# Folding a per-head matrix into projection weights: products of 120 rows by 128 columns, and quarters of 60 by 64

## The chip, the cores and the metric

The kernel runs on one core of a Trainium2 chip. The metric is the device time of one execution in microseconds (us). Engines are named as in the profile: PE is TensorE (PEld its weight loads), DVE is VectorE, ACT is ScalarE, POOL is GpSimd, SP is SyncE, which issues the DMAs.

## What is computed

Two layers, each a linear attention and a dense block, on x of 2048 rows by 640 columns with 32 heads of 20. Of the reference, what matters here:

```python
q, k, v = split(layernorm(x) @ wqkv)              # per head: S x 20
pq = einsum("bhsd,hdf->bhsf", q, w_phi)           # the same 20 x 20 matrix per head
pk = einsum("bhsd,hdf->bhsf", k, w_phi)           # for queries and for keys
phi_q = concat([softmax(pq), softmax(-pq)])       # phi_k likewise
o = phi_q (phi_k^T v) / (phi_q phi_k^T 1 + 1e-6)
x = x + o @ wo
x = x + mish(layernorm(x) @ w1 + b1) @ w2
```

Since `(n @ W) @ w_phi` is `n @ (W @ w_phi)`, the kernel multiplies w_phi into the query and key weights once, at the start of the first layer. Softmax does not change when a constant is taken off a row, so the last of the 20 columns of each head is subtracted from the other 19 (`DL` = 19), and 32 x 19 = 608 columns are left.

## The kernel before, in words

**Blocks.** x is worked in 8 blocks of 256 rows, two tiles of 128 each. For each block the first attention stage makes keys (`k0`, `k1`), values (`v0`, `v1`) and queries (`q0`, `q1`), each by `project`: for each of five 128-row slices of the weights three F32R products (high x high, high x low, low x high), in two halves of columns. Every weight is therefore held as a rounded high part and a low part, the rest.

**The folds.** `load_raw` loads the transposed query or key weights as six tiles: t = 0 to 3 with 120 rows (six heads), t = 4 and 5 with 80 (four heads). `fold_part` (L248) multiplies, for slice k and tile t, the 120 x 128 piece of raw weights with the block-diagonal w_phi (`bd`) in F32; three tiles t fill one bank of PSUM, c = 0 with 18 heads and c = 1 with 14. `fold_end` takes a bank out: ACT rounds it to the high part (L261), DVE subtracts to get the low part (L262), 342 columns for c = 0 and 266 for c = 1. `shift_phi` (L255, POOL) does the subtraction of the last column in `bd`. There are 5 x 6 products for queries and as many for keys (`fold_phi`).

**The value weights.** They are loaded by `fetch_v` (L183) and split by ACT (L140, high) and DVE (L141, low part, 640 columns), one slice after another: slices 0 to 4.

**The statistics.** `norm_stats` takes, for each tile of an x block, two BNStats (L281, 320 columns each) and an aggregate (L283); POOL and DVE make scale and offset (L290, L291, L293). ACT normalizes (L129, L132), PE transposes (L311), ACT and DVE make high and low parts (L129 or L132, L317).

**After a projection** of queries or keys, `features` copies it out (L132), reduces maximum and minimum per head (L400), subtracts (L401, L403), takes Exp on ACT (L132), sums per head on DVE (L409), inverts (L410) and multiplies on POOL (L411). Queries are then transposed by DVE (L456) and stored (L460). The products of keys and values are L448.

**What sets the order.** The first stage, up to the query projection of tile 0 and the splits of the values, is written out by hand (`with written():` in `attend_first`): the order of these instructions among themselves on each engine is the program's. All else is placed by a planner, which puts each instruction in its engine's queue by its own model of times; it can put an instruction of its own between those written by hand. Each engine then runs its queue strictly in that order. All loads and stores go through one queue, SP's, and take turns on eight completion semaphores: in the built program each waits until the DMA eight places before it has landed. Two PSUM tags are used here: `mm` (two banks, 2 buffers) and `one` (one bank, 4 buffers).

Of the kernel before, what the change touches and what calls it, by code (L numbers as in the profile page):

```python
# [8 lines left out]
F32 = mybir.dt.float32  # L9
F32R = mybir.dt.float32r  # L10
AF = mybir.ActivationFunctionType
ALU = mybir.AluOpType
# [4 lines left out]
P = 128  # L17
S = 2048
D = 640
F = 1536  # L20
H = 32
DH = 20
DL = DH - 1
KD = D // P
# [7 lines left out]
QK = H * DL  # L32
# [3 lines left out]
VW = H * (DH + 1)  # L36
SKEW = 2
LAYERS = 2
LN_EPS = 1e-5
DEN_EPS = 1e-6  # L40
E_CAP = 65536.0
# [3 lines left out]
def kernel(  # L45
# [13 lines left out]
    nc = tc.nc  # L59
# [3 lines left out]
    wts = ctx.enter_context(tc.tile_pool(name="wts", bufs=1))  # L63
# [116 lines left out]
    def fetch_v(k):  # L180

        st = (row_tile, row_tile, v_tile, v_tile, big_tile)[k]()[:, :D]
        nc.sync.dma_start(st, wv[k * P:(k + 1) * P, :])  # L183
        return st
# [42 lines left out]
    def load_raw(which, ts=range(6)):  # L227

        raw = []
        for t in ts:  # L230
            rows = 120 if t < 4 else 80
            if t < 5:
                r = wts.tile([P, D], F32, tag=f"r2{'hl'[which]}{5 + t}", name=f"raw{which}{t}")
            else:
                r = r2_wide(10 + which, F32)[:, 0]

            n = P if t < 5 else rows
            c0 = which * D + (t * 120 if t < 5 else D - rows)
            nc.sync.dma_start(r[:n], wqk_t[c0:c0 + n, :])
            raw.append((r, rows))  # L240
        return raw

    def fold_part(ps, k, t, bd, raw):

        r, rows = raw[t]
        heads = rows // DH
        n = DL * (6 * (t % 3) if t < 5 else 10)
        nc.tensor.matmul(ps[:, n:n + heads * DL].rearrange("p (j d) -> p j d", d=DL), r[:rows, k * P:(k + 1) * P],  # L248
                         bd[:rows, t, :rows].rearrange("p (j d) -> p j d", d=DH)[:, :, :DL], start=True, stop=True)

    def shift_phi(bd, ts):

        b = bd[:, ts].rearrange("p t (j d) -> p (t j) d", d=DH) if isinstance(ts, slice) else (
            bd[:80, ts, :80].rearrange("p (j d) -> p j d", d=DH))
        nc.gpsimd.tensor_tensor(b[:, :, :DL], b[:, :, :DL], b[:, :, DL:].to_broadcast([b.shape[0], b.shape[1], DL]),  # L255
                                op=ALU.subtract)

    def fold_end(ws, ps, k, c):
        n0, n1 = (0, 18 * DL) if c == 0 else (18 * DL, QK)
        hi, lo = ws[k][0][:, n0:n1], ws[k][1][:, n0:n1]  # L260
        nc.scalar.activation(hi, ps[:, :n1 - n0], AF.Copy)  # L261
        nc.vector.tensor_tensor(lo, ps[:, :n1 - n0], hi.bitcast(F32), op=ALU.subtract)  # L262

    def fold_phi(ws, bd, raw):

        pss = {}
        for k, c in ((0, 0), (1, 0), (2, 0), (3, 0), (0, 1), (1, 1), (2, 1), (3, 1), (4, 0), (4, 1)):
            if c == 0:
                mm = None if k % 2 else mm_tile()
                pss[k] = [one_tile(), one_tile()] if k % 2 else [mm[:, 0], mm[:, 1]]  # L270
            ps = pss[k][c]
            for t in range(3 * c, 3 * c + 3):
                fold_part(ps, k, t, bd, raw)
            fold_end(ws, ps, k, c)


    def norm_stats(t, xt):
# [136 lines left out]
    def fetch(x_src, b, xt=None):  # L414
        xt = x_tile() if xt is None else xt
        nc.sync.dma_start(xt, row_block(x_src, b))
        return xt

    def attend_first(layer, x_src, first):
# [58 lines left out]
        if first is None:  # L478
            with written():
                xt = fetch(x_src, 0)  # L480
                bd = big_tile()[:120, :720].rearrange("p (t c) -> p t c", t=6)
                nc.sync.dma_start(bd[:, :3], phi_bd[:, :3])
                raw_q = load_raw(0, range(3))

                nc.vector.memset(bd[:80, 5, :80], 0.0)
                nc.sync.dma_start(bd[:40, 5, :40], phi_bd[80:120, 4, 80:120])
                nc.sync.dma_start(bd[40:80, 5, 40:80], phi_bd[:40, 5, :40])
                nc.sync.dma_start(bd[:, 3:5], phi_bd[:, 3:5])
                shift_phi(bd, slice(0, 3))
                raw_q += load_raw(0, range(3, 6))  # L490
                kv_ws = [r1_pair(k) for k in range(KD)]
                raw_v = [fetch_v(k) for k in range(KD)]
                raw = load_raw(1)
                early = fetch(x_src, 1)
                mvs = [norm_stats(t, xt) for t in range(BT)]
                norm_scale(0, mvs)
                shift_phi(bd, slice(3, 5))
                shift_phi(bd, 5)

                q_ws = [r2_pair(k) for k in range(KD)]  # L500
                mm = [mm_tile(), mm_tile()]
                pcs = [mm[0][:, 0], mm[0][:, 1], mm[1][:, 0], mm[1][:, 1], one_tile()]
                for t in range(3):
                    for k in range(KD - 1):
                        fold_part(pcs[k], k, t, bd, raw_q)
                fold_end(q_ws, pcs[0], 0, 0)
                xn = [row_tile() for _ in range(BT)]
                act(xn[0], xt[:, 0, :], AF.Identity, bias=stats[:, 0, 1, 0:1], scale=stats[:, 0, 0, 0:1])
                nc.vector.tensor_scalar(xn[1], xt[:, 1, :], stats[:, 0, 0, 1:2], stats[:, 0, 1, 1:2],
                                        op0=ALU.mult, op1=ALU.add)  # L510
                fold_end(q_ws, pcs[1], 1, 0)
                fold_end(q_ws, pcs[2], 2, 0)
                nxt = Transposed(xn)
                nxt.step()
                fold_end(q_ws, pcs[3], 3, 0)
                nxt.step()
                for t in range(3):
                    fold_part(pcs[4], 4, t, bd, raw_q)
                nxt.step()
                fold_end(q_ws, pcs[4], 4, 0)  # L520
                mm = mm_tile()
                q0 = [mm[:, 0], mm[:, 1], mm]
                project_half(q0[0], nxt, 0, q_ws, 0, 0, w=QC)

                def make_v(k):
                    split(kv_ws[k][0][:, D:2 * D], kv_ws[k][1][:, D:2 * D], raw_v[k])

                for k in range(KD):
                    ps = one_tile()
                    for t in range(3, 6):  # L530
                        fold_part(ps, k, t, bd, raw_q)
                    fold_end(q_ws, ps, k, 1)
                    if k > 0:
                        make_v(k - 1)
                project_half(q0[1], nxt, 0, q_ws, 0, 1, w=QC)
                make_v(KD - 1)
            nc.sync.dma_start(mask, bass.AP(tensor=head_mask.tensor, offset=head_mask.offset,
                                            ap=[[1, 120], [120 * (DH + 1), 3]]))
        else:
            nxt, kv_ws = first  # L540
            load_k_weights(kv_ws)
            q_ws = load_q_weights()
        for b in range(NB):
# [351 lines left out]
    with tc.block(schedule_with_timeline_sim=True):  # L895
        src, first = x, None
        for layer in range(LAYERS):
            last = layer == LAYERS - 1
            dst = out if last else x2_d
# [39 lines left out]
            src = dst  # L939
# [38 lines left out]
```

## Time and profile before

| | us |
|---|---|
| median of three runs (1368.06 to 1368.76) | 1368.17 |
| the profiled execution | 1368.56 |
| its span | 1366.8 |
| PE busy | 1351.2 |
| DVE busy | 1075.5 |
| ACT busy | 578.4 |
| POOL busy | 452.6 |

In rows of groups the columns are line, engine, operation, tile written and tiles read, shape and count, then busy time and the mean in ns of one, then the idle time of the engine ahead of them and what ended it. In rows of the timeline they are start, length, engine, line and instruction, and in brackets the idle time before it. Starts are counted from the start of the span. Products overlap on PE, so the difference of two starts says more than a length.

### The profile page before, as it was taken

The page shows a single profiled execution, that of the slowest core. Times are in us where ns is not written, and L with a number is a line of the kernel's source. Part 1 is how long each engine was busy: PE and PEld are TensorE (multiplying, and loading weights), DVE is VectorE, ACT ScalarE, POOL GpSimd, SP SyncE. Part 2 cuts the span into 40 slices and gives each one's busy share as a digit, 9 for nine tenths or more (in the row PEclk, how much of TensorE's full clock was granted, in tenths as well). Part 3 has the DMA queues.
Part 4 walks back from the last instruction along what each step waited for, and adds up shares of the span by engine and source line. Part 5 has one row for each costly group of instructions (what it writes and reads, how often), then busy time and mean ns, then how long its engine had stood idle before and what let it go on. Part 6 is the DMA issues. An engine that isn't in the chain of part 4 may idle for free. (4 is left out here: it accounts for less than half of the span.)

```text
span 1366.8 us, 30959 instructions
## 1 busy us (share of the span) xinstructions
PE 1351.2 (99%) x12896; PEld 1337.9 (98%) x12896; DVE 1075.5 (79%) x1822; ACT 578.4 (42%) x970; POOL 452.6 (33%) x401
## 2 busy tenths in 40 slices
PE   9999999999999999999999999999999999999998
PEld 9999999999999999999999999999999999999998
DVE  6888988876787888778769898989668776677775
ACT  5444444212454544455444333432235444444443
POOL 2355554434222222122235444544252211111112
PEclk9999999999999999999999999999999999999999
DMA  9533333798714443334563433458974221333200
GB/s 343 150 81 64 74 60 78 213 282 273 223 36 93 116 117 84 57 94 113 151 218 75 83 60 70 86 132 267 287 251 136 78 71 35 90 97 97 77 21 20
DMA packets 350469, 169.19 MB, mean 124 GB/s; under 512 B 287209, under 2 KB 323801, under 8 KB 350329
## 3 DMA queue, kind: packets, MB, share of 16 engines
q1 hardware_dynamic: 350329, 167.22, 45.4%
q8 instruction: 101, 1.65, 0.5%
q14 instruction: 39, 0.32, 0.1%
HBM read 104.59 MB, written 62.59 MB: 122 GB/s over the span
## 5 line engine op out<-in xcount | busy, mean ns | idle before, releaser
L816 PE MATMUL mm<-r2h,ol 128*128 128x320 f32 x1280 | 304.9, 309 | 0.0
L800 POOL TENSOR_TENSOR ol<-big,ol 128x512 fp32r<-128x512 f32 (+1 forms) x98 | 131.2, 1338 | 477.2 <-ACT ol L799 419.1
L774 PE MATMUL one<-xtl,r1h 128*128 128x256 f32 x960 | 268.2, 279 | 0.0
L774 PE MATMUL one<-xth,r1l 128*128 128x256 f32 x960 | 268.0, 279 | 0.0
L774 PE MATMUL one<-xth,r1h 128*128 128x256 f32 x960 | 265.9, 279 | 0.0
L816 PEld LDWEIGHTS mm<-r2h,ol 128*128 128x128 f32 x1280 | 219.2, 188 | 0.0
L816 PE MATMUL mm<-r2l,ol 128*128 128x320 f32 x640 | 197.3, 309 | 0.0
L375 PE MATMUL mm<-r1h,xth 128*128 128x304 f32 (+1 forms) x600 | 185.4, 309 | 2.2 <-DVE r1l L262 1.5
L375 PE MATMUL mm<-r1h,xtl 128*128 128x304 f32 (+1 forms) x600 | 183.6, 307 | 2.0 <-DVE xtl L317 1.8
L375 PE MATMUL mm<-r1l,xth 128*128 128x304 f32 (+1 forms) x600 | 183.8, 306 | 0.0
L774 PEld LDWEIGHTS one<-xtl,r1h 128*128 128x128 f32 x960 | 180.4, 188 | 0.0
L774 PEld LDWEIGHTS one<-xth,r1l 128*128 128x128 f32 x960 | 180.4, 188 | 0.0
L774 PEld LDWEIGHTS one<-xth,r1h 128*128 128x128 f32 x960 | 179.6, 188 | 0.0
L789 DVE TENSOR_SCALAR big<-big 128x512 f32<-128x512 f32 (+1 forms) x98 | 56.9, 581 | 110.2 <-ACT big L787 110.0
L411 POOL TENSOR_TENSOR r<-r,r 128x1280 f32<-128x1280 f32 x32 | 79.1, 2473 | 131.7 <-DVE r L410 124.1
L816 PEld LDWEIGHTS mm<-r2l,ol 128*128 128x128 f32 x640 | 120.2, 188 | 0.0
L791 ACT ACTIVATE big<-big,two 128x512 f32<-128x512 f32 (+1 forms) x98 | 70.2, 716 | 116.2 <-DVE big L790 116.2
L787 ACT ACTIVATE big<-one,b1s 128x256 f32<-128x256 f32 x192 | 80.9, 468 | 88.8 <-PE one L774 88.3
L799 ACT ACTIVATE ol<-big 128x512 fp32r<-128x512 f32 (+1 forms) x98 | 60.9, 622 | 134.5 <-DVE big L798 134.4
L375 PEld LDWEIGHTS mm<-r1h,xth 128*128 128x128 f32 x600 | 112.8, 188 | 3.9 <-DVE r1l L262 1.7
L375 PEld LDWEIGHTS mm<-r1h,xtl 128*128 128x128 f32 x600 | 112.7, 188 | 2.7 <-DVE xtl L317 2.7
L375 PEld LDWEIGHTS mm<-r1l,xth 128*128 128x128 f32 x600 | 112.8, 188 | 0.1
(136 smaller groups left out, 3125.0 us busy)
## 6 DMA issues: line engine op xcount, KB each, us to landing
e_d<-r SPq DMA_DIRECT2D x128, 160.0 KB, 4.0
big<-e_d SPq DMA_DIRECT2D x32, 640.0 KB, 7.4
x_d<-xt SPq DMA_DIRECT2D x23, 640.0 KB, 4.6
xt<-x_d SPq DMA_DIRECT2D x22, 640.0 KB, 5.5
n_d<-xn SPq DMA_DIRECT2D x176, 80.0 KB, 2.2
xt<-in_x SPq DMA_DIRECT2D x16, 640.0 KB, 4.0
xn<-x_d SPq DMA_DIRECT2D x28, 320.0 KB, 4.4
v<-n_d SPq DMA_DIRECT2D x30, 256.0 KB, 3.0
```

What stands on the lines that cost most here:

```text
L375: nc.tensor.matmul(ps[:, :w], a[:, sl], r, start=(k == 0 and n == 0), stop=(k == KD - 1 and n == 2))
L411: nc.gpsimd.tensor_tensor(eg, eg, r.unsqueeze(2).to_broadcast([P, 2 * H, DH]), op=ALU.mult)
L774: nc.tensor.matmul(ph[:, j, :], l, r, start=(n == 0), stop=(n == 3 * KD - 1))
L787: exps[0] = nc.scalar.activation(part(ta, 0)[:, j - js.start], ph[:, j, :], AF.Exp, bias=b1s[:, 2 * pr + j:2 * pr + j + 1]).ins
L789: nc.vector.tensor_scalar_min(e, e, E_CAP)
L791: nc.scalar.activation(r, n, AF.Ln, bias=two)
L799: nc.scalar.activation(ah[:, js], n, AF.Copy)
L800: nc.gpsimd.tensor_tensor(al[:, js], n, ah[:, js].bitcast(F32), op=ALU.subtract)
L816: nc.tensor.matmul(pys[t][:, c, :HC], l[:, j, sl], r, start=(f == 0 and n == 0), stop=(f == KF - 1 and n == 2))
```

## The change

The 30 products each of queries and keys become 30 sets of four: two slots s of at most three heads (60 rows), at rows 0 and 64 of the raw tile, and two halves q of 64 columns. The four use the four 64 x 64 quarters of the array. Slot s writes bank s of a pair, half q writes partitions 64q to 64q + 63.

- `FOLD` lists, for each tile t, first head and number of heads of both slots.
- `load_raw` loads two times 64 rows for each t (for the last key tile 64 and 40): 12 loads in place of 6.
- `load_phi` loads w_phi as blocks of 60 x 60 (fewer heads at the end) into `bd`, which is zeroed first (128 x 360): 4 loads for c = 0 and 6 for c = 1, in place of 1 and 3.
- `pair_banks` takes two `one` banks or one `mm` tile in turn. `fold_end` takes out an `mm` pair by one instruction each on ACT and DVE (342 or 266 columns) and two `one` banks by two each (171 or 133).
- `shift_phi` is two instructions of 9 x 19 columns in place of 18 x 19, 12 x 19 and 4 x 19.

The orders of the built programs differ only in the first stage and the folds of the keys; from the second key projection (`k1` of block 0) on, PE's are the same. On DVE, from the first low part of the queries' c = 1 on (st = BNStats, ag = aggregate, of the x block whose number follows; lq = low part of queries, slice k; sv = split of values; lk = low part of keys; a number after x is how many pieces):

```
before: lq0 lq1 sv0 lq2 sv1 lq3 sv2 lq4 sv3 sv4 lk(0,0) st1x4 ag1x2 st2x2 max,min(q0) st2x2 ...
after:  lq0x2 lq1 sv0 lq2x2 st1x3 sv1 st1 ag1 lq3 sv2 ag1 st2x2 lq4x2 sv3 st2x2 sv4 ag2 ... max,min(q0) ... st3x4 sum(q0) lk(0,0) ...
```

On PE, before, the three products of the first key fold stand among the last query folds and the rest between `v1` and the key projection of tile 0, the last inside it; after, all ten groups stand between `v1` and that projection, and the transposes of x block 1 behind them.

The diff, cut to its core:

```diff
+FOLD = (((0, 3), (9, 3)), ((3, 3), (12, 3)), ((6, 3), (15, 3)), ((18, 3), (25, 3)), ((21, 3), (28, 2)), ((24, 1), (30, 2)))
...
-            n = P if t < 5 else rows
-            c0 = which * D + (t * 120 if t < 5 else D - rows)
-            nc.sync.dma_start(r[:n], wqk_t[c0:c0 + n, :])
+            for s, (h, _) in enumerate(FOLD[t]):
+                c0 = which * D + h * DH
+                n = min(64, 2 * D - c0)
+                nc.sync.dma_start(r[64 * s:64 * s + n], wqk_t[c0:c0 + n, :])
...
+    def load_phi(bd, c):
+        def block(s, t, h, n, m=1):
...
+        for args in (((0, 0, 0, 3, 2), (0, 2, 6, 3), (1, 0, 9, 3), (1, 1, 12, 3, 2)) if c == 0 else
+                     ((0, 3, 18, 3), (1, 3, 25, 3), (0, 4, 21, 3), (1, 4, 28, 2), (0, 5, 24, 1), (1, 5, 30, 2))):
+            block(*args)
...
     def fold_part(ps, k, t, bd, raw):
-        nc.tensor.matmul(ps[:, n:n + heads * DL].rearrange("p (j d) -> p j d", d=DL), r[:rows, k * P:(k + 1) * P],
-                         bd[:rows, t, :rows].rearrange("p (j d) -> p j d", d=DH)[:, :, :DL], start=True, stop=True)
+        for s, (h, heads) in enumerate(FOLD[t]):
+            n0 = DL * (h % 9 if t < 3 else h - 18 - 7 * s)
+            rows = slice(64 * s, 64 * s + max(2, heads) * DH)
+            rhs = bd[rows, t, :heads * DH].rearrange("p (j d) -> p j d", d=DH)[:, :, :DL]
+            for q in range(2):
+                nc.tensor.matmul(ps[s][64 * q:64 * q + 64, n0:n0 + heads * DL].rearrange("p (j d) -> p j d", d=DL),
+                                 raw[t][rows, k * P + 64 * q:k * P + 64 * q + 64], rhs, start=True, stop=True)
...
     def fold_end(ws, ps, k, c):
+        if len(ps) > 2:
+            parts = [(slice(n0, n0 + 2 * w), ps[2][:, :, :w])]
+        else:
+            parts = [(slice(n0 + s * w, n0 + (s + 1) * w), ps[s][:, :w].unsqueeze(1)) for s in range(2)]
+        for cs, src in parts:
+            n = src.shape[1]
+            hi, lo = (ws[k][i][:, cs].rearrange("p (s d) -> p s d", s=n) for i in range(2))
+            nc.scalar.activation(hi, src, AF.Copy)
+            nc.vector.tensor_tensor(lo, src, hi.bitcast(F32), op=ALU.subtract)
...
     def fold_phi(ws, bd, raw):
-        for k, c in ((0, 0), (1, 0), (2, 0), (3, 0), (0, 1), (1, 1), (2, 1), (3, 1), (4, 0), (4, 1)):
+        for k in range(KD):
+            for c in range(2):
+                ps = pair_banks((k + c) % 2)
...
-                bd = big_tile()[:120, :720].rearrange("p (t c) -> p t c", t=6)
-                nc.sync.dma_start(bd[:, :3], phi_bd[:, :3])
+                bd = big_tile()[:, :360].rearrange("p (t c) -> p t c", t=6)
+                nc.vector.memset(bd, 0.0)
+                load_phi(bd, 0)
                 raw_q = load_raw(0, range(3))
+                load_phi(bd, 1)
+                shift_phi(bd, 0)
                 raw_q += load_raw(0, range(3, 6))
```

More of the change, by code (lines that the diff above doesn't have):

```diff
@@ L230, in load_raw @@
         for t in ts:
-            rows = 120 if t < 4 else 80
-            if t < 5:
-                r = wts.tile([P, D], F32, tag=f"r2{'hl'[which]}{5 + t}", name=f"raw{which}{t}")
-            else:
-                r = r2_wide(10 + which, F32)[:, 0]
-            n = P if t < 5 else rows
-            c0 = which * D + (t * 120 if t < 5 else D - rows)
-            nc.sync.dma_start(r[:n], wqk_t[c0:c0 + n, :])
-            raw.append((r, rows))
-        return raw
-    def fold_part(ps, k, t, bd, raw):
[L245 to L248, printed above, removed]
-                         bd[:rows, t, :rows].rearrange("p (j d) -> p j d", d=DH)[:, :, :DL], start=True, stop=True)
@@ L251, in shift_phi @@
[L251 to L256, printed above, removed]
-    def fold_end(ws, ps, k, c):
[L259 to L262, printed above, removed]
@@ L264, in fold_phi @@
-    def fold_phi(ws, bd, raw):
-        pss = {}
-        for k, c in ((0, 0), (1, 0), (2, 0), (3, 0), (0, 1), (1, 1), (2, 1), (3, 1), (4, 0), (4, 1)):
[L268 to L274, printed above, removed]
+            r = (wts.tile([P, D], F32, tag=f"r2{'hl'[which]}{5 + t}", name=f"raw{which}{t}") if t < 5 else
+                 r2_wide(10 + which, F32)[:, 0])
@@ new lines, in load_raw @@
+            for s, (h, _) in enumerate(FOLD[t]):
+                c0 = which * D + h * DH
+                n = min(64, 2 * D - c0)
+                nc.sync.dma_start(r[64 * s:64 * s + n], wqk_t[c0:c0 + n, :])
+            raw.append(r)
+        return raw
+    def load_phi(bd, c):
+        def block(s, t, h, n, m=1):
+            a, j = divmod(h, 6)
+            src = phi_bd[DH * j:DH * (j + n), a, DH * j:DH * (j + n)]
+            dst = bd[64 * s:64 * s + DH * n, t:t + m, :DH * n]
+            if m > 1:
+                step = 60 * (phi_bd.ap[0][0] + 1) if j == 0 else None
+                src = bass.AP(tensor=src.tensor, offset=src.offset, ap=[src.ap[0], [step, m], src.ap[-1]])
+                nc.sync.dma_start(dst, src)
+            else:
+                nc.sync.dma_start(dst[:, 0], src)
+        for args in (((0, 0, 0, 3, 2), (0, 2, 6, 3), (1, 0, 9, 3), (1, 1, 12, 3, 2)) if c == 0 else
+                     ((0, 3, 18, 3), (1, 3, 25, 3), (0, 4, 21, 3), (1, 4, 28, 2), (0, 5, 24, 1), (1, 5, 30, 2))):
+            block(*args)
@@ new lines, in shift_phi @@
+    def shift_phi(bd, c):
+        b = bd[:, 3 * c:3 * c + 3].rearrange("p t (j d) -> p (t j) d", d=DH)
+        nc.gpsimd.tensor_tensor(b[:, :, :DL], b[:, :, :DL], b[:, :, DL:].to_broadcast([P, 9, DL]), op=ALU.subtract)
+    def fold_end(ws, ps, k, c):
+        n0, w = (0, 9 * DL) if c == 0 else (18 * DL, 7 * DL)
+        if len(ps) > 2:
[7 more added lines that the diff above has]
+            nc.vector.tensor_tensor(lo, src, hi.bitcast(F32), op=ALU.subtract)
@@ L277, in norm_stats, with pair_banks @@
+    def pair_banks(single):
+        if single:
+            return [one_tile(), one_tile()]
+        mm = mm_tile()
+        return [mm[:, 0], mm[:, 1], mm]
+    def fold_phi(ws, bd, raw):
+        for k in range(KD):
+            for c in range(2):
+                ps = pair_banks((k + c) % 2)
+                for t in range(3 * c, 3 * c + 3):
+                    fold_part(ps, k, t, bd, raw)
+                fold_end(ws, ps, k, c)
     def norm_stats(t, xt):
@@ L480, in attend_first @@
                 xt = fetch(x_src, 0)
-                bd = big_tile()[:120, :720].rearrange("p (t c) -> p t c", t=6)
-                nc.sync.dma_start(bd[:, :3], phi_bd[:, :3])
+                bd = big_tile()[:, :360].rearrange("p (t c) -> p t c", t=6)
+                nc.vector.memset(bd, 0.0)
+                load_phi(bd, 0)
                 raw_q = load_raw(0, range(3))
[L485 to L489, printed above, removed]
+                load_phi(bd, 1)
+                shift_phi(bd, 0)
                 raw_q += load_raw(0, range(3, 6))
@@ L496, in attend_first @@
                 norm_scale(0, mvs)
-                shift_phi(bd, slice(3, 5))
-                shift_phi(bd, 5)
+                shift_phi(bd, 1)
                 q_ws = [r2_pair(k) for k in range(KD)]
-                mm = [mm_tile(), mm_tile()]
-                pcs = [mm[0][:, 0], mm[0][:, 1], mm[1][:, 0], mm[1][:, 1], one_tile()]
+                pcs = [pair_banks(k < 2) for k in range(KD - 1)]
                 for t in range(3):
@@ L516, in attend_first @@
                 nxt.step()
+                ps = pair_banks(True)
                 for t in range(3):
-                    fold_part(pcs[4], 4, t, bd, raw_q)
+                    fold_part(ps, KD - 1, t, bd, raw_q)
                 nxt.step()
-                fold_end(q_ws, pcs[4], 4, 0)
+                fold_end(q_ws, ps, KD - 1, 0)
                 mm = mm_tile()
@@ L528, in attend_first @@
                 for k in range(KD):
-                    ps = one_tile()
+                    ps = pair_banks(k % 2 == 0)
                     for t in range(3, 6):
```

## The prediction

> **What bounds the kernel now.** I read the page first, then the groups of the first 45 us, then the timeline of each engine there, since everything that the change touches lies before 45 us.
>
> ```profile
> PE 1351.2 (99%) x12896; PEld 1337.9 (98%) x12896; DVE 1075.5 (79%) x1822; ACT 578.4 (42%) x970; POOL 452.6 (33%) x401
> ```
>
> PE is busy for 1351.2 of 1366.8 us. After the first stage it has next to no idle time to give, so what that stage gains or loses reaches the end undiminished. The groups of TensorE in the first 45 us:
>
> ```profile
> L248 PE MATMUL mm<-big,raw 120*128 120x114 f32 (+1 forms) x54 | 7.5, 277 | 0.2 <-DVE r1l L262 0.2
> L248 PE MATMUL one<-big,raw 120*128 120x114 f32 (+1 forms) x46 | 6.7, 273 | 0.0
> ...
> L92 PE MATMUL one<-ident 128*128 128x128 f32 x30 | 5.6, 371 | 1.3 <-POOL ident masks.py:199 1.3
> ...
> L375 PE MATMUL mm<-r1h,xth 128*128 128x304 f32 x10 | 3.1, 313 | 1.5 <-DVE r1l L262 1.5
> ...
> L311 PE MATMUL one<-ident,xn 128*128 128x128 f32 x20 | 3.1, 278 | 0.9 <-ACT xn L129 0.9
> L248 PE MATMUL one<-big,r 80*128 80x76 f32 x14 | 2.7, 275 | 0.0
> L248 PE MATMUL mm<-big,r 80*128 80x76 f32 x6 | 1.2, 275 | 0.0
> ```
>
> The folds are L248: 54 + 46 + 14 + 6 = 120 records for 60 products in F32, so each product is two instructions. PE idles only 0.9 and 1.5 us there, both times for another engine.
>
> **The products.** The rate is read from starts, not durations, since products overlap:
>
> ```profile
> 29.91 0.82 PE L248 MATMUL one<-big,raw 120*128 120x114 f32 x6
> 30.57 0.83 PE L248 MATMUL mm<-big,raw 120*128 120x114 f32 x6
> ...
> 64.50 0.83 PE L448 MATMUL one<-big,v 128*21 128x40 f32 x64
> 65.26 0.66 PE L311 MATMUL one<-ident,xn 128*128 128x128 f32 x4
> ...
> 252.72 1.38 PE L652 MATMUL mm<-kvb,big 120*64 120x63 f32 x40
> 253.94 0.27 PE L652 MATMUL mm<-kvb,ol 80*64 80x42 f32 x4
> 254.03 1.36 PE L652 MATMUL mm<-kvb,big 120*64 120x63 f32 x40
> ```
>
> Three products take 30.57 - 29.91 = 0.66 us, or 0.22 each, and all 60 take 13.2. L652 writes two halves of 64 columns in turn: 44 instructions in 254.03 - 252.72 = 1.31 us, so 0.060 for a product that two tiles share. L448 writes four column tiles in turn: 64 instructions in 0.76 us, so 0.024 per product. Cost falls with the number of column tiles; row tiles side by side are in no row here. If four quarters run at once, a set of four costs two turns of L652's pair, 2 x 0.060 = 0.12 us; if only the two column halves do, 4 x 0.060 = 0.24. All 60 sets then cost 7.2 or 14.4 us: a gain of 6.0 or a loss of 1.2. I take 7.2, since L448 shows that more tiles give more.
>
> [...]
>
> **Does that gain reach the end?** It would if PE bounded the whole stage. The built order of instructions says otherwise. VectorE now, from the timeline:
>
> ```profile
> 17.55 0.82 DVE L141 TENSOR_TENSOR r1l<-xn,r1h 128x640 fp32r<-128x640 f32 x1 [0.19 <-ACT r1h L140]
> ...
> 20.45 0.43 DVE L262 TENSOR_TENSOR r2l<-one,r2h 128x266 fp32r<-128x266 f32 x1
> 20.79 0.82 DVE L141 TENSOR_TENSOR r1l<-v,r1h 128x640 fp32r<-128x640 f32 x1
> 21.52 0.82 DVE L141 TENSOR_TENSOR r1l<-big,r1h 128x640 fp32r<-128x640 f32 x1
> 22.26 0.51 DVE L262 TENSOR_TENSOR r1l<-mm,r1h 128x342 fp32r<-128x342 f32 x1
> 23.10 1.67 DVE L281 BATCH_NORM_STATS2 bn<-xt 128x6 f32<-128x320 f32 x4 [0.33 <-DMA xt<-in_x]
> ```
>
> L141 is the low part of the value weights, five "splits", done at 21.52 + 0.82 = 22.34. Only then come the statistics L281 of x block 1, which waited 0.33 us for their load. In the changed kernel the planner sets three of these statistics **ahead of split 1** (counting from 0), and two of block 2 ahead of split 3 and two ahead of split 4. VectorE runs in order: when it comes there, at about 18.6 (split 0 ends at 18.37, then one low part), it holds until x block 1 has landed. Behind it stand the low parts of queries 3 and 4 and splits 1 to 4, which PE needs for the rest of q, v0 and v1.
>
> **When does that load land?** It is the 23rd load in SyncE's queue now and the 41st after.
>
> ```profile
> DMA  0036999999999999999999999999999999999999
> ...
> 0.72 0.39 SPq L416 DMA_DIRECT2D xt<-in_x  x1
> 1.17 0.47 SPq L482 DMA_DIRECT2D big<-in_phi_bd  x1
> 1.69 1.29 SPq L239 DMA_DIRECT2D raw<-in_wqk_t  x3
> ...
> 8.92 0.90 SPq L183 DMA_DIRECT2D v<-in_wv  x2
> ...
> 10.35 3.35 SPq L239 DMA_DIRECT2D raw<-in_wqk_t  x5
> 14.20 0.33 SPq L239 DMA_DIRECT2D r<-in_wqk_t  x1
> 15.02 0.33 SPq L416 DMA_DIRECT2D xt<-in_x  x1
> ```
>
> The first row is the DMA load over 0 to 25 us in 40 slices: full from 3 us on. From the start to that x block the shapes give 6.94 MB now and 6.96 after (phi blocks 0.16 less, the last tiles of q and k 0.18 more), so it lands no earlier for its bytes: 23.07 now. More loads can only delay it. Each issue holds SyncE for some 0.44 us (two in 0.90, three in 1.29), and by the built order each load waits until the eighth before it has landed. Ten of the first 17 are now small phi blocks, 2 to 28 KB, which take turns from the eight: in steps of 0.44 the six of the second half are issued from about 6.0 to 8.3, so the next raw load goes out at 8.7, against 4.76 now, and the DMA engines run dry for up to 2.5 us. Against that, halves of 64 rows go evenly over 16 engines, and the best stretch may be kept longer. Bounds: 22.5 (the hole hidden by that) and 26.5 (hole kept, and 40 issues x 0.44 binding). I take **24.3**.
>
> **The sum, behind T = 24.3.** VectorE's steps: statistics 1.67 / 4 = 0.42; split 21.52 - 20.79 = 0.73; low part of 266 20.79 - 20.45 = 0.34, of 133 about 0.21 (the 0.51 and 0.43 of 342 and 266 give 1.05 ns an element); a small aggregate about 0.16. In the new order: 3 x 0.42 + 0.73 + 0.42 + 0.16 + 0.34 + 0.73 + 0.16 + 0.84 + 2 x 0.21 + 0.73 + 0.84 + 0.82 = 7.4. The last split ends at 31.7, against 22.34.
>
> ```profile
> 29.98 0.74 ACT L132 ACTIVATE v<-one 128x320 f32<-128x320 f32 x2
> 30.61 1.26 ACT L132 ACTIVATE r<-r 128x1280 f32<-128x1280 f32 x1
> ...
> 31.91 1.49 DVE L409 TENSOR_REDUCE r<-r 128x64 f32<-128x1280 f32 x1 [1.49 <-ACT r L132]
> 33.31 0.50 DVE L262 TENSOR_TENSOR r1l<-one,r1h 128x342 fp32r<-128x342 f32 x1
> ...
> 35.94 2.36 POOL L411 TENSOR_TENSOR r<-r,r 128x1280 f32<-128x1280 f32 x1 [5.79 <-DVE r L410]
> ...
> 38.42 0.41 PE L375 MATMUL mm<-r1h,xth 128*128 128x304 f32 x1 [1.49 <-DVE r1l L262]
> ...
> 43.40 0.30 PE L375 MATMUL mm<-r2h,xth 128*128 128x304 f32 x1
> 43.54 0.30 PE L375 MATMUL mm<-r2l,xth 128*128 128x304 f32 x1
> xt<-in_x SPq DMA_DIRECT2D x16, 640.0 KB, 4.0
> ```
>
> PE has 33 products of v0 and v1 queued behind split 4, at about 0.145 (0.14 from 43.40 to 43.54 for 304 columns): 36.6, and 36.9 with the last one's tail. ScalarE queues the eviction of v1 (half of 0.74) and then the Exp of query tile 0 (1.26): 38.6. On VectorE the reduction L409 stands behind that and behind four statistics of the next x block; its load is released once ScalarE has normalized block 1, about 34.9, and takes about 3.4 to 4.0: 38.5, and 1.5 more for statistics gives 40.0. The reduction ends at 41.4; now the key folds' low parts start at 33.31. They cost 3 x 0.42 + 4 x 0.26 + 2 x 0.34 + 6 x 0.21 = 4.2 (now 3.8 for five of 0.42 and five of 0.34), with about 2.6 of reciprocal, transpose and small pieces between, and the transpose waits for POOL's L411 (2.36) with some 1.7 uncovered: the last ends near 50. PE's last folds wait for banks until some 48.4; it starts the transposes of block 1 at 48.8 and the first key projection at 49.3, against 38.42. That projection is 30 x 0.14 + 0.5 of transposes, so the query projection after it starts at 54.1, against 43.40, and two more transposes (0.2) stand behind it. From there both PE orders are the same. **Loss 10.9 us.**
>
> The query folds are not in this sum: they end near 16.7, where PE then waits some 7 us anyway, and the key folds wait for VectorE. That is where the 6.0 us go; if that cover were gone, they would be gained. Zeroing 360 columns instead of 80 (0.12 now) hides behind the 4 us of x block 0.
>
> The profiled run took 1368.56, 1.76 beyond its span of 1366.8; with 10.9 more it is 1379.5. The median of the three runs, 1368.17, is 0.4 below it: **1379.1**.
>
> **Rivals.**
> - *The load is early* (other side). If x block 1 landed before 18.6, VectorE would not hold, and PE would keep its gain: up to 6.0, less 0.2 to 2 for longer evictions, so 1362 to 1367, taken as 1364. For it: nothing but the smaller phi blocks. Against it: the full DMA row and 23.07 now. The point of decision is a landing at 18.6. 4%.
> - *Quarters share only two ways.* Then the change does not do what it says, and the folds cost 14.4; but they lie in waits, and only the last key folds show: 0.1 to 0.5 more, 1379.4. 6%.
> - *The clock falls.* L92 and L311 are the same transpose, 371 and 278 ns in mean: the first 30 ran before PE was warm. A hold of 7 us and a gap of 3 to 4 us among the key folds could bring that back: for 30 products at 93 ns more, 2.8 us; I take 2, since PE waits in part of that time anyway: 1381. No pause in this trace is that long. [...] 22%.
> - *The load is later*, at 26.5: 1381.3, and with the clock 1383. 14%.
> - *No difference*, two of these cancelling: 2%. The forecast itself: 52%, 1377 to 1381 for T from 22.5 to 26.
>
> The range is 1375 to 1385: the forecast's lowest 1377 and the late load with the slow clock, 1383, with 2 us at either end for what I mis-size behind T. A measurement of this kernel can tell about 0.2%. Faster 4%, same 2%, slower 94%.
>
> **What would show it.** Right: VectorE idle for 4 to 7 us from about 18 to 19 us with x as the releaser, ahead of a statistics instruction; PE idle after its first products of v0; the first key projection near 49; products of 64x57 in sets of about 0.12 us. Wrong: x block 1 landing before 19; a hold shorter than 3 us; folds that PE waits for nowhere and a first key projection before 40; a loss that goes on after 60 us.

## The result and the profile after

| | before | after |
|---|---|---|
| time, median of 4 runs each | 1368.23 us (1368.06 to 1368.76) | 1389.11 us (1387.10 to 1389.69) |
| the profiled execution: time, span | 1368.56, 1366.8 us | 1388.74, 1387.0 us |
| first key projection starts | 38.42 us | 59.15 us |

The medians differ by 20.9 us, where a loss of 10.9 was forecast. The ratio on record is 1.0138 (95% interval 1.0126 to 1.0150), or 18.9 us; the two medians themselves give 1.0153. The record does not say which runs the ratio takes, so the loss is known to some 2 us. The loss is all there by 60 us: the first key projection starts 20.7 us later. These are groups of TensorE in the first 65 us (busy time and mean ns, then the idle time before them and who ended it):

```profile
L265 PE MATMUL one<-big,raw 60*64 60x57 f32 (+1 forms) x216 | 8.1, 256 | 4.3 <-DVE r1l L283 2.6 <-DMA raw<-in_wqk_t 1.6
L399 PE MATMUL one<-r1l,xth 128*128 128x320 f32 x20 | 6.6, 341 | 12.1 <-DVE r1l L142 12.1
...
L265 PE MATMUL mm<-big,raw 60*64 60x57 f32 (+1 forms) x184 | 5.7, 241 | 4.6 <-DVE r1l L283 4.0 <-DVE r2l L283 0.6
```

PE stands 12.1 us in v0 for a value split's low part (L142, L141 before), then 6.6 us (2.6 + 4.0) among the key folds for low parts (L283, L262 before). Both are VectorE's; its timeline tells why:

```profile
21.19 0.49 DVE L283 TENSOR_TENSOR r2l<-one,r2h 128x133 fp32r<-128x133 f32 x2
33.44 1.28 DVE L305 BATCH_NORM_STATS2 bn<-xt 128x6 f32<-128x320 f32 x3 [11.77 <-DMA xt<-in_x]
34.64 0.81 DVE L142 TENSOR_TENSOR r1l<-xn,r1h 128x640 fp32r<-128x640 f32 x1
...
39.70 0.81 DVE L142 TENSOR_TENSOR r1l<-big,r1h 128x640 fp32r<-128x640 f32 x1
...
47.99 1.67 DVE L305 BATCH_NORM_STATS2 bn<-xt 128x6 f32<-128x320 f32 x4 [2.72 <-DMA xt<-in_x]
49.58 1.47 DVE L433 TENSOR_REDUCE r<-r 128x64 f32<-128x1280 f32 x1
50.97 0.50 DVE L283 TENSOR_TENSOR r1l<-mm,r1h 128x342 fp32r<-128x342 f32 x1
...
59.11 0.48 DVE L283 TENSOR_TENSOR r1l<-one,r1h 128x133 fp32r<-128x133 f32 x2
```

Three statistics of x block 1 (L305) stand ahead of split 1 and hold VectorE for 11.77 us, until that block lands at 33.4. The other splits follow, then the statistics of block 3 hold it for 2.72 us more, and only then do the key folds' low parts begin, at 50.97 against 33.31. On PE, the folds themselves went as hoped, and the projections behind them:

```profile
45.90 0.57 PE L265 MATMUL mm<-big,raw 60*64 60x57 f32 x24
46.29 0.41 PE L265 MATMUL one<-big,raw 60*64 60x57 f32 x16
46.52 0.30 PE L265 MATMUL one<-big,r 40*64 40x38 f32 x8
46.62 0.57 PE L265 MATMUL one<-big,raw 60*64 60x57 f32 x24
...
59.15 0.60 PE L399 MATMUL mm<-r1h,xth 128*128 128x304 f32 x1
59.55 0.46 PE L399 MATMUL mm<-r1l,xth 128*128 128x304 f32 x1
59.80 0.46 PE L399 MATMUL mm<-r1h,xtl 128*128 128x304 f32 x1
...
65.20 0.39 PE L399 MATMUL mm<-r2h,xth 128*128 128x304 f32 x1
```

24 instructions, three sets of four quarters, take 46.29 - 45.90 = 0.39 us, so 0.13 a set (0.117 between starts within a run) against 0.22 for a whole product. The key projection runs at 0.25 us a product (59.80 - 59.55) where 0.14 was usual, and takes 6.06 us to the query projection (65.20 - 59.15) against 4.98 before (43.40 - 38.42). The windows (last three columns: granted clock, DMA share, GB/s) name the reason:

```profile
25.00:30.00 5.00, 0.00 (x0) 0.00 (x0) 0.00 (x0) 0.00 (x0) 0.00 (x0) 0.82 0.95 264
30.00:35.00 5.00, 0.00 (x0) 0.00 (x0) 1.56 (x4) 0.00 (x0) 0.00 (x0) 0.50 0.90 238
...
55.00:60.00 5.00, 2.41 (x27) 2.34 (x28) 3.68 (x9) 1.22 (x4) 0.81 (x1) 0.50 0.40 82
```

With the pauses the clock fell to 0.50. And SyncE's queue of DMA issues, with its windows from the trace of after and then of before, shows why x came late:

```profile
3.06 3.74 SPq L237 DMA_DIRECT2D raw<-in_wqk_t  x6
6.84 2.61 SPq L252 DMA_DIRECT2D big<-in_phi_bd  x6
9.49 3.77 SPq L237 DMA_DIRECT2D raw<-in_wqk_t  x4
...
27.29 0.33 SPq L440 DMA_DIRECT2D xt<-in_x  x1
```
```profile
8.00:12.00 4.00, 2.44 (x81) 1.75 (x72) 1.85 (x6) 2.17 (x6) 0.70 (x4) 0.89 0.36 93
...
24.00:28.00 4.00, 0.00 (x0) 0.00 (x0) 0.00 (x0) 0.26 (x1) 0.00 (x0) 1.00 1.02 268
```
```profile
8.00:12.00 4.00, 3.09 (x26) 2.79 (x26) 2.19 (x6) 2.48 (x6) 1.06 (x5) 1.00 1.05 328
...
16.00:20.00 4.00, 4.00 (x36) 4.00 (x35) 3.32 (x7) 3.72 (x9) 0.16 (x1) 1.00 1.06 362
```

A half load of 64 rows holds SyncE 3.74 / 6 = 0.62 us, against 0.43 for a whole one. Behind the six phi loads the DMA engines are idle most of 8 to 12 us (share 0.36). And where they are full, mostly with raw key loads (24 to 28 us after, 16 to 20 before), they move 268 GB/s against 362. The x load is issued at 27.29 in place of 15.02.

### The profile page after: what moved, and what is told of

It is laid out like the page before. It is cut to its first block, busy times and chain, and to the rows that moved or that the text cites. A ratio compares the mean times of both kernels' runs of the same rounds, so it can differ in the third digit from the quotient of the medians.

```text
span 1387.0 us, 31723 instructions
## 1 busy us (share of the span) xinstructions
PE 1353.3 (98%) x13256; PEld 1339.1 (97%) x13256; DVE 1075.8 (78%) x1833; ACT 579.8 (42%) x981; POOL 451.5 (33%) x400
```

## The experiments

My theory: x block 1 lands late because of the loads in halves and pieces; what the planner set behind its statistics makes that a loss. Rivals: the quarters or their evictions in two pieces cost the time; VectorE's order alone does; the late loads alone do. T is the time at which VectorE takes up x block 1; differences are medians against the kernel before on the same chip.

| run | T | first key projection | against before | ratio, 95% interval |
|---|---|---|---|---|
| after | 33.4 | 59.15 | +20.9 | 1.0138 (1.0126 to 1.0150) |
| e1 order of blocks 1, 2 | 32.7 | 57.74 | +19.2 | 1.0140 (1.0123 to 1.0157) |
| e13 order of blocks 1, 2, 3 | 32.5 | 51.30 | +13.1 | 1.0098 (1.0081 to 1.0115) |
| e8 phi restored | 29.3 | 55.78 | +16.4 | 1.0116 (1.0102 to 1.0130) |
| e10 raw restored (one run) | 25.4 | 55.26 | +16.9 | none |
| e5 both restored | 22.8 | 51.37 | +13.3 | 1.0097 (1.0082 to 1.0113) |
| e6 e5 and order of 1, 2 | 22.6 | 45.59 | +7.1 | 1.0052 (1.0038 to 1.0065) |
| e7 e5 and order of 1, 2, 3 | 22.9 | 39.20 | +2.0 | 1.0012 (1.0004 to 1.0021) |
| e11 e7, key folds earlier | 23.5 | 41.71 | +2.1 | 1.0012 (1.0002 to 1.0022) |
| e12 before, key folds earlier | 24.4 | 36.51 | -0.6 | 0.9996 (0.9988 to 1.0005) |
| e4 before, halves by rows | 28.6 | 45.91 | +7.3 | 1.0055 (1.0040 to 1.0070) |
| e14 before, halves interleaved | 28.8 | 46.49 | +6.6 | 1.0048 (1.0033 to 1.0063) |
| e9 before, halves by columns | 26.3 | 42.09 | +2.5 | 1.0018 (1.0006 to 1.0029) |

The ratios are not the quotients of these medians in every row, so rows that differ by less than 2 us, as after and e1 do, are not told apart. Outside e11 and e12, the first key projection's delay (38.42 as zero) gives the time within 1.5 us: what happens before it decides. (In e11 and e12 all or most of v1 stands behind the folds, so their starts compare with no other run's.) The planner orders each kernel anew: in e5 and e10, for one, it sets statistics ahead of split 0, where after has them ahead of split 1.

### Order alone: e1, then e13

e1, on the changed kernel (`last_low` is the last value split's low part, kept by `split`):

```diff
-            norm_scale(b, [norm_stats(t, xt) for t in range(BT)])
+            with (tc.issue_after(last_low[0]) if b < 3 else ExitStack()): norm_scale(b, [norm_stats(t, xt) for t in range(BT)])
```

> The changed kernel with one edit: VectorE's statistics of x blocks 1 and 2 are queued behind its last value split, as the kernel before has them. Loads, quarters and evictions are as in the changed kernel, so x block 1 should still land near 33 us. Theory (late loads times VectorE's order): the hold of 11.8 us ahead of split 1 goes, PE does v0 and v1 some 12 us earlier (near 30), but the low parts of the key folds stay behind the statistics of blocks 1 to 3, which still wait for their loads; the first key projection starts near 53 in place of 59.2 and the time is 1381 to 1384. Rival (the order alone is the cause, the late loads would be hidden): first key projection near 39, time 1366 to 1370. Rival (products or two-piece evictions cost the time): no change, 1387 to 1390.

It gave 1388.13, near "no change", though not for the reason of that rival. VectorE, in e1:

```profile
25.63 0.83 DVE L142 TENSOR_TENSOR r1l<-big,r1h 128x640 fp32r<-128x640 f32 x1 [0.71 <-ACT r1h L141]
32.72 1.67 DVE L305 BATCH_NORM_STATS2 bn<-xt 128x6 f32<-128x320 f32 x4 [6.26 <-DMA xt<-in_x]
...
46.34 1.67 DVE L305 BATCH_NORM_STATS2 bn<-xt 128x6 f32<-128x320 f32 x4 [4.09 <-DMA xt<-in_x]
47.93 1.47 DVE L433 TENSOR_REDUCE r<-r 128x64 f32<-128x1280 f32 x1
49.32 0.20 DVE L307 BATCH_NORM_AGGREGATE mv<-bn 128x2 f32<-128x12 f32 x1
49.43 0.46 DVE L283 TENSOR_TENSOR r1l<-mm,r1h 128x342 fp32r<-128x342 f32 x1
```

The last split is done at 26.5 in place of 40.5, but the key folds' low parts begin at 49.43 in place of 50.97, since block 3's statistics stand ahead of them until 46.34. The wait moved. My number was wrong by 4 to 7 us: the expectation names that block's statistics, but leaves too little for the wait until 46.34. e13 queues its statistics behind the last low part too (`last_key`, kept by `fold_end`):

```diff
-            with (tc.issue_after(last_low[0]) if b < 3 else ExitStack()): norm_scale(b, [norm_stats(t, xt) for t in range(BT)])
+            with (tc.issue_after((last_low if b < 3 else last_key)[0]) if b < 4 else ExitStack()): norm_scale(b, [norm_stats(t, xt) for t in range(BT)])
```

> The changed kernel with its own loads (x block 1 near 33 us), and the statistics of x blocks 1 and 2 queued behind the last value split and those of block 3 behind the last low part of the key folds: the order of the run with restored loads that came within 2 us of the kernel before, now with late loads. Holding back blocks 1 and 2 alone gave 1388.1. Theory (that run gained nothing because block 3's statistics, ahead of the key folds' low parts, then held VectorE until 46.3): first key projection at 49 to 53 in place of 57.7, time 1380 to 1384. Rival (block 3 does not matter; with late loads the holds on ScalarE decide): 1387 or more.

1382.07, first key projection at 51.30, both in the theory's range. With late loads, the order is worth 59.15 - 51.30 = 7.9 us, and 12.9 us of delay remain.

### One load with two runs: e2, e3

e2 loads a tile in one DMA of 128 rows that are two runs of 64; e3 is e2 with e1's order.

```diff
+            one = bass.AP(tensor=wqk_t.tensor, offset=wqk_t[c0:c0 + 64, :].offset, ap=[[gap, 2], [D, 64], [1, D]])
-                nc.sync.dma_start(r[64 * s:64 * s + n], wqk_t[c0:c0 + n, :])
+                nc.sync.dma_start(r, one)
```

> The changed kernel with one edit: each tile of raw query and key weights comes in one load of 128 rows (two runs of 64 rows, one descriptor list) in place of two loads of 64 rows; only the last key tile keeps two. The ten small phi loads stay, and so does an order on VectorE in which statistics of x block 1 stand ahead of value splits (now four of them, ahead of split 0). Theory (the half loads made x block 1 late: 0.6 us of SyncE for each and a lower rate): x block 1 lands at 24 to 25 in place of 33.4, the first key projection starts at 49 to 51, time 1378 to 1381, which is what the prediction gave for T = 24.3. Rival (ten phi loads are what delays): landing at 31 or later and time above 1385. Rival (products or two-piece evictions): no change, 1387 to 1390.

> The changed kernel with both edits: one load for each raw tile, and the statistics of x blocks 1 and 2 queued behind the last value split. The quarters and their evictions in two pieces are unchanged. Theory: VectorE holds only after its splits, x block 1 lands at 24 to 25, first key projection at 38 to 41, time 1366 to 1371. If the quarters' shorter folds (6 us of PE less) reached the end at all it would be below 1366. Rival (products or two-piece evictions cost most of the loss): 1380 or more.

1447.68 (1.0577, 1.0562 to 1.0593) and 1441.80 (1.0534, 1.0518 to 1.0549): a miss, and no test of the theory, for the edit slowed what it was to restore: VectorE takes up x block 1 at 86.2 and 87.5 us. A window of e2 in which only such loads run:

```profile
50.00:60.00 10.00, 0.00 (x0) 0.00 (x0) 0.00 (x0) 0.00 (x0) 0.00 (x0) 0.50 0.13 51
```

A DMA share of 0.13 is what 2 busy engines of 16 would make (0.125); 51 GB/s were moved. Why such a load runs at that rate is shown by no run. Later kernels have the rows laid out by the host instead.

### Loads restored, then the order: e5, e6, e7

In e5 the host arranges each raw tile's 128 rows, and phi in its new blocks, so that they come in twelve loads and two, of 128 rows each:

```diff
-            for s, (h, _) in enumerate(FOLD[t]):
...
-                nc.sync.dma_start(r[64 * s:64 * s + n], wqk_t[c0:c0 + n, :])
+            c0 = (6 * which + t) * P
+            nc.sync.dma_start(r, wqk_t[c0:c0 + P, :])
...
+        nc.sync.dma_start(bd[:, 3 * c:3 * c + 3], phi_bd[:, 3 * c:3 * c + 3])
```

> The changed kernel with its loads restored and nothing else: the host lays the query and key weights out so that each tile is one load of 128 contiguous rows on all 16 engines, and w_phi so that it is two loads of 128 rows (no zeroing). Quarters, evictions in two pieces and the planner's preference for statistics ahead of value splits stay (block 1 now ahead of split 0, block 2 ahead of splits 1 and 2). Theory (late landing and VectorE's order together): x block 1 lands at 22.5 to 24, VectorE holds from about 17.5 until then, the last split ends 7.5 us later near 31, the first key projection starts at 46 to 49, time 1375 to 1380. Rival (the late loads alone are the cause): x block 1 early is enough, time 1366 to 1370. Rival (products or evictions in pieces): 1385 or more.

1382.90, or +13.3: better by 7.6 us than the changed kernel's +20.9. That is not all of the loss, though T is back at 22.8, even before 23.1. Early loads alone do not heal it. The range was missed by 3 us, as block 3's statistics again hold VectorE until 40.7. e6 adds e1's order and e7 that of e13:

> As the run with restored loads, and the statistics of x blocks 1 and 2 queued behind the last value split on VectorE; those of block 3 still stand ahead of the key folds' low parts, which in the kernel before they do not. Theory: splits end near 22.5, VectorE then waits for x block 3 (released by the normalization of block 1, landing at 32 to 34), the key folds' low parts start near 36, first key projection at 41 to 44, time 1370 to 1374. Rival (late loads alone): as with restored loads alone, 1366 to 1370.

> As the run before it in this list, and the statistics of x block 3 queued behind the last low part of the key folds as well: VectorE's order is then about that of the kernel before, with quarters as the only difference left. Theory: first key projection at 36 to 39, time 1365 to 1369. If the products' 6 us reach the end, 1362 to 1365. Rival (products or evictions in pieces cost): 1372 or more.

e6: 1376.69, first key projection at 45.59, above my ranges by 2.7 and 1.6 us. e7: 1371.55, first key projection at 39.20: 2.5 us above the theory's range, at the edge of the rival's. Order is worth 51.37 - 39.20 = 12.2 us with early loads; late loads are worth 51.30 - 39.20 = 12.1 us with the good order, and 59.15 - 51.37 = 7.8 with the planner's. The two overlap: **neither cure alone gives more than 7.9 of the 20.7 us, both together give 20.0.** (The planner's order with early loads is that of e5, which is not quite after's.) What is left in e7, on PE and by the windows:

```profile
32.81 0.91 PE L265 MATMUL mm<-big,raw 60*64 60x57 f32 x24 [2.75 <-DVE r1l L283]
...
39.20 0.60 PE L399 MATMUL mm<-r1h,xth 128*128 128x304 f32 x1
39.60 0.46 PE L399 MATMUL mm<-r1l,xth 128*128 128x304 f32 x1
```
```profile
35.00:40.00 5.00, 3.71 (x85) 3.53 (x80) 3.77 (x11) 2.24 (x7) 1.58 (x3) 0.50 0.89 288
```

PE pauses 2.75 us among the key folds, its clock falls, and the key projection starts at 0.25 us a product. The start 0.8 us later and 1.1 more to the query projection (45.32 - 39.20 = 6.1, against 4.98), at the lower clock, make the 2.0. Quarters and evictions in two pieces are both still in e7; no run takes them apart, so which of them keeps the 2.0 us is not shown.

### Does the quarters' gain show anywhere? e11, e12

Both write the key folds ahead of the second value projection, so that PE has its products to do while they are evicted; e11 on e7, e12 on the kernel before:

```diff
+                if b == 0 and n == 2 and layer == 0: fold_phi(kv_ws, bd, raw)
                 if b == 0 and n == (1 if layer else 3):
-                    if layer == 0:
-                        fold_phi(kv_ws, bd, raw)
```

> Quarters with restored loads and VectorE's order as in the kernel before (1371.55 in an earlier run), and the key folds written ahead of the second value projection in place of behind it, so that PE has 4.8 us of products to do while ScalarE and VectorE evict them. Theory (the folds' gain lay in waits, and the pause among the key folds let PE's clock fall): no pause above 1.5 us there, first key projection at 34 to 36.5, full clock, time 2 to 4 us below the kernel before. Rival (evictions in pieces bound the folds in any place): no better than 1369.

> The kernel before with the same one edit: key folds written ahead of the second value projection, whole products of 120 by 128. The control of the run above: theory, PE has 6.6 us of key folds to do here in place of 3.6, so it gains less: first key projection at 36.5 to 38, time 0 to 2 us below the kernel before. If this gains as much as the quarters do, the gain there is the order's, not the quarters'.

e11: 1371.71, e12: 1369.07. The expectation for e11 failed, and its rival (no better than 1369) came; e12 is as expected, and its ratio can't be told from 1. PE in e11, from its first key fold:

```profile
24.34 0.57 PE L265 MATMUL mm<-big,raw 60*64 60x57 f32 x24
24.74 0.40 PE L265 MATMUL one<-big,raw 60*64 60x57 f32 x16
24.96 0.29 PE L265 MATMUL one<-big,r 40*64 40x38 f32 x8
25.07 0.55 PE L265 MATMUL one<-big,raw 60*64 60x57 f32 x24
25.44 0.40 PE L265 MATMUL mm<-big,raw 60*64 60x57 f32 x16
25.66 0.29 PE L265 MATMUL mm<-big,r 40*64 40x38 f32 x8
31.65 0.90 PE L265 MATMUL mm<-big,raw 60*64 60x57 f32 x24 [5.70 <-DVE r1l L283]
```

Four groups of 24 instructions (two of them in pieces of 16 and 8) fill four pairs of banks in 1.6 us; then PE waits 5.70 us for a low part to free a pair. PE runs in order, so v1 behind the folds can't fill that. In e12, with one bank a group, PE has no pause over 0.5 us from 11.1 to 42 us. But the planner's order differs there too: 28 of the value products stand between the first fold groups and the last ones, where in e11 all of them stand behind all ten groups. So in e11 the quarters' speed was spent on reaching a wait sooner; whether two banks a group or the order of v1 makes that wait was not tried apart.

### What makes the loads late: e8, e10, e4, e14, e9

e8 restores the phi loads alone, e10 the raw loads alone, on the changed kernel (diffs: the halves of e5's).

> The changed kernel with only the phi loads restored (two loads of 128 rows, laid out by the host, no zeroing); raw tiles still come in two loads of 64 rows. Theory: x block 1 lands at 29 to 30 in place of 33.4 (28.6 in the kernel before with half loads alone, which has two loads fewer), and as VectorE's order has statistics ahead of the splits, the time moves with it: 1383 to 1386. Rival (the phi loads only fill a hole that is hidden): 33 us and 1387 to 1390.

> The changed kernel with only the raw loads restored (one load of 128 contiguous rows for each tile, laid out by the host); the ten phi loads stay. Asked is the landing of x block 1, as both counts of the four cases (33.4 with both kinds of small loads, 29.3 with half raws alone, 22.8 with neither). If the two delays add, it lands at 26.5 to 27.5; if the phi loads cost only because half raws follow them, at 23 to 24.5. VectorE's order here has statistics of blocks 1 and 2 ahead of split 0, so the time is 12 to 18 us above the kernel before.

T: 33.4 with both kinds of small loads, 29.3 without phi's, 25.4 without the halves, 22.8 without either. Phi's pieces cost 2.6 to 4.1 us, the halves 6.5 to 8.0. e10's T lies between its two predictions. One by one the two cost 2.6 and 6.5, together 10.6: each makes the other some 1.5 us worse.

The kernel before, with halves alone (e4), tells what late loads cost where VectorE's order is sound:

```diff
-            nc.sync.dma_start(r[:n], wqk_t[c0:c0 + n, :])
+            for p in range(0, n, 64): nc.sync.dma_start(r[p:min(n, p + 64)], wqk_t[c0 + p:c0 + min(n, p + 64), :])
```

> The kernel before with one edit: each tile of raw weights comes in two loads (64 rows and the rest). Products, evictions and phi loads are those of the kernel before; its statistics stand behind the splits. Theory: x block 1 lands at 28 to 32 in place of 23.1, and as the key folds' low parts stand behind its statistics the first key projection moves by about as much: time 1373 to 1378. Rival (half loads are hidden, only the order matters): 1367 to 1369.5.

T 28.6, 1376.23, both in the theory's ranges: late loads make 7.3 us of time with no quarter in the kernel. But not through x block 1 alone, as the expectation has it. In this kernel the first key fold stands among the last query folds, and PE waits for its raw key tiles three times there, 3.7 us in all. ScalarE and VectorE take that fold out ahead of the last splits:

```profile
23.61 0.74 PE L248 MATMUL mm<-big,raw 120*128 120x114 f32 x2 [2.10 <-DMA raw<-in_wqk_t]
...
24.39 0.46 ACT L261 ACTIVATE r1h<-mm 128x342 fp32r<-128x342 f32 x1 [3.89 <-PE mm L248]
...
27.40 0.82 DVE L141 TENSOR_TENSOR r1l<-big,r1h 128x640 fp32r<-128x640 f32 x1
28.58 1.67 DVE L281 BATCH_NORM_STATS2 bn<-xt 128x6 f32<-128x320 f32 x4 [0.36 <-DMA xt<-in_x]
```

The last split is done at 28.2 in place of 22.3, and VectorE then waits only 0.36 us for x. So late key tiles delay the splits (5.9 us) about as much as x block 1 is late (5.5). In the changed kernel all key folds stand behind v1, and no fold waits for a key tile.

Two reasons for the lateness remained: a low rate for 64 partitions, or the number of loads and issues. e9 splits by columns (`r[:n, p:p + HC]`), e14 puts one half into the even partitions and the other into the odd ones (`r[s:n:2]`, rows in that order by the host):

> The kernel before with one edit: each tile of raw weights comes in two loads of all its rows by 320 of 640 columns (1280-byte rows), so as many loads as with halves of 64 rows, and the same bytes, but each still spread over up to 128 partitions. If it is the number of loads (SyncE's issue, eight in flight) that delays x block 1, it lands at 27 to 29 as with halves by rows (28.6), time 1374 to 1378. If it is that a load of 64 rows fills only half the partitions and goes at a lower rate, it lands at 23 to 24.5, time 1367.5 to 1370.5.

> The kernel before with each raw tile in two loads of 64 rows of 2560 bytes, as in the run with halves by rows (x block 1 at 28.6, 1376.2), but one load fills the even partitions and the other the odd ones (the host has the rows in that order), so each load spreads over all 128 partitions. If the low rate of the halves comes from filling only one half of the partitions at a time, packets take 100 to 120 ns in place of 150 to 170 and x block 1 lands at 24 to 26.5, time 1369 to 1373. If it comes from a load having only 64 rows (four packets on each engine), packets stay at 150 or more, it lands at 28 to 29, time 1375 to 1377.

e9: T 26.3, between both predictions; 1372.20. e14: T 28.8 and 1375.62, as its second prediction had them, but not for that reason: its packets of 2560 bytes took 102 ns (median of 20 to 24 us, 167 in e4), as the first one had them. The windows of e4 and then of e14 tell more:

```profile
8.00:12.00 4.00, 2.69 (x20) 2.15 (x18) 1.25 (x4) 1.51 (x4) 1.08 (x6) 1.00 1.07 239
...
20.00:24.00 4.00, 1.03 (x6) 0.71 (x5) 1.70 (x3) 0.50 (x1) 0.00 (x0) 0.67 1.06 249
```
```profile
8.00:12.00 4.00, 2.81 (x24) 2.45 (x23) 2.45 (x6) 2.27 (x5) 1.20 (x6) 1.00 0.72 207
...
20.00:24.00 4.00, 1.75 (x5) 1.29 (x6) 0.74 (x2) 0.00 (x0) 0.00 (x0) 0.50 0.68 208
```

In e4 the engines are full (1.07, 1.06) and move only 239 and 249 GB/s, against 328 and 362 in the windows of before shown above: rows that go to 64 neighbouring partitions go slowly. Spread over all partitions (e14), the engines are no longer full in these windows (0.72, 0.68), and T is as late: now SyncE's queue holds the loads back. Six loads of 64 rows in a row hold it 0.62 to 0.63 us each, in e4 and e14 alike, but six of 128 rows by half the columns 0.45 (e9). These are SyncE's rows of e14 and of e9:

```profile
1.69 3.77 SPq L239 DMA_DIRECT2D raw<-in_wqk_t  x6
...
13.29 9.19 SPq L239 DMA_DIRECT2D raw<-in_wqk_t  x10
```
```profile
1.69 2.72 SPq L239 DMA_DIRECT2D raw<-in_wqk_t  x6
```

Issuing is not the whole of it: of the 9.19 us for ten key loads in e14, 3.0 are waits for loads eight places ahead. So there are two limits at about the same height, the rate into 64 partitions and the queue (its issues and its eight places), and lifting one leaves the other; the queue's two parts were not tried apart. Why rows to 64 neighbouring partitions move at the lower rate (e4: 249 GB/s with the engines full, against 362 in the kernel before) is not shown. For the longer issue I found no reason either; it stays open.

## Why the prediction was wrong in size and right in kind

- **The products**: right. 0.12 us a set was taken, 0.117 to 0.13 measured; all four quarters share the array. That the gain would lie in waits was right too; with the folds moved, in e11, it still does.
- **VectorE's hold** ahead of split 1: right in place and cause. It began at 21.7 us (33.44 - 11.77), where 18.6 was named, and lasted 11.77 us, where 4 to 7 were.
- **The landing of x block 1** is the step that failed: T = 24.3 (bounds 22.5 to 26.5), measured 33.4. Three parts of it were off. "Each issue holds SyncE for some 0.44 us" was read from loads of 128 rows; loads of 64 take 0.62 each in a row. "Halves of 64 rows go evenly over 16 engines, and the best stretch may be kept longer": with all engines full (share 1.02) they moved 268 GB/s (249 in e4) where 362 was had. The hole of up to 2.5 us was there (share 0.36 for 4 us, so 2.6), and the lower bound had let the halves cover it. Of the 10.6 us between T in e5 and in the changed kernel, phi's pieces are 2.6 to 4.1 and the halves 6.5 to 8.0; how the halves' share divides between rate and issue is open.
- **The sum behind T**: right. It gave 25.0 us from T to the first key projection; 59.15 - 33.44 = 25.7. The chain of statistics, low parts and splits up to the last split was put at 7.4 and took 40.5 - 33.4 = 7.1. With T = 33.4 the same sum gives 1379.1 + 9.1 = 1388.2, against 1389.11.
- **The clock**, a rival at 22%: it did fall. The first key projection took 1.1 us more to the query projection (6.06 against 4.98), where I had 2; its twelve products at 0.25 in place of 0.14 alone make 1.3, for before's 4.98 has some key folds in it. After pauses of PE of 12.11 and 4.01 us the grant was 0.50, and in e7 it was 0.50 after a pause of 2.75 us. From 10 to 15 us its mean was 0.61, where no pause of PE is over 0.9 us. How long a pause has to be for the clock to fall is shown by no run.
- **Range and other rivals**: 1375 to 1385 missed by 4 us, since both bounds of T were built from the costs that before's loads show: neither allowed a lower rate or a longer issue than theirs. The early load and sharing two ways did not come.

## What to carry to other kernels

A smaller tile of a product may force its operands into smaller loads: price the loads by their partitions and rows, not by bytes, before the product (here 64 rows a load: 249 GB/s and 0.62 us an issue, against 362 and 0.43 for 128). Where an engine that runs in order is given work that waits for a transfer, ask what stands behind it; here, late loads and a poor order each hid the other's cure, and only both edits together gave the time back. A product that gets faster but takes two banks in place of one may only reach the wait for its evictions sooner (5.70 us in e11).

## What I had not expected of the hardware

- 64 rows of 2560 bytes to neighbouring partitions: 239 to 249 GB/s with the engines full, against 328 to 362 for 128 rows (e4, before).
- In a row, the issue of such a load holds SyncE 0.62 us, that of 128 rows 0.43 to 0.45, also when these carry the same bytes (e4, before, e9).
- Loads of 128 rows from two runs of 64 in the source ran at a DMA share of 0.13, as 2 of 16 engines would, at 51 GB/s (e2).
- Four quarters at four places of the array (60 rows by 64 columns, 57 columns moving) take 0.117 us in F32 (after); one whole product of 120 by 128 with 114 moving took 0.22 (before).
